# Attention, experts and a gated layer on one core: first pair's swapped keys, the experts' table and sixteen transposes moved or added

## The chip, the cores and the metric

The kernel runs on one core of a Trainium2 chip. The metric is the device time of one execution in microseconds; the profile is that of one execution of the same program. TensorE is called PE, its weight loads PEld, VectorE DVE, ScalarE ACT, GpSimd POOL and SyncE SP; "SPq" is the queue from which SP starts DMAs.

## The reference

Three stages follow each other: attention that keeps scores near the row's maximum, a layer in which each token goes to one of eight experts, and a gated layer. Sizes: batch 4, 8 heads, 576 tokens, head dimension 64; 2304 tokens of width 512; experts 512 to 1024 to 512; gated layer 512 to 1536 to 512.

```python
scores = q @ k.T / sqrt(64)
scores = where(scores >= max(scores) - tau, scores, -1e9)
x = softmax(scores) @ v                       # (2304, 512) after the heads are joined
logits = x @ w_gate
e = argmax(logits); g = softmax(logits)[e]
y = g * (relu(x @ w1[e]) @ w2[e])
out = ((y @ w_a) * (y @ w_b)) @ w_out
```

Every product is done in fp32r in two halves: a value is split into a high part (a cast to fp32r) and a low part (the value minus the high part), and three of the four partial products are summed.

## The kernel before, in words

**Attention** (class `Attention`) goes over 16 pairs of heads, i = 0 to 15: heads p and p + 4 of batch b lie in the two halves of the 128 partitions. For each pair q and k come as raw tiles of 9 blocks of 64 columns (`load`; the first pair in `__init__`, lines 296 to 298): eight blocks of the first 512 tokens and a tail with the last 64 tokens of both heads. `split_units` casts them to a high part (lines 417 to 421) and subtracts a low part (line 428). `qk_units` transposes the result on PE (lines 460, 484, 485), and ACT or DVE copies the banks into the tiles `qT` and `kT` (lines 472 to 478, 490 to 496). `kT` is kept twice, the second copy with the high and the low half of the partitions exchanged; `swap` (line 466) makes it with a DMA from the first copy. A pair then has nine score tiles, g = 9i to 9i + 8 (`s_units`): product on PE (line 677), row maximum on DVE (690), a threshold per two tiles (694), exponential on ACT (698), mask and row sum on DVE (710). `pv_units` transposes the masked weights (785), splits them (735 to 750), multiplies by v (861) and brings the heads back into rows (887).

**The gate.** After each batch `gate` computes logits, the expert of each token, its rank among the tokens of that expert (a product with a triangle matrix, lines 1002 to 1006, unit `tr`), its row in the scratch `xs` (unit `slot`, lines 1020 to 1027) and the new row counts (unit `base`, line 1037), scales the rows (`xg`) and scatters them with indirect DMAs on POOL's queue (unit `sc`, line 44). Before that, 32 zero fills (`z`, line 398) clear the rows of `xs` that may stay empty.

**The lead expert.** After three batches `lead_select` (from line 505) picks the fullest expert. Its first 256 rows are computed inside attention's last pair and behind it (`lead_units`, units `l_*`: weights, first products at line 601, second products at line 625), which gives PE work while the last gate runs.

**The order** of all of this is written out by hand: the string `ORDER` (lines 68 to 231) names every unit, and `emit` issues them in that order, so that each engine and each DMA queue gets its instructions as the string has them.

**The experts** (class `Experts`). `order` (lines 1299 to 1331) takes the counts, sorts the experts by size and builds the table `ti` with each place's expert, first output column, count and first row in `xs`; `chunk_count` computes from it how many extra chunks there are. SP, ACT and DVE read the table's values into registers (line 1605). With them SP loads an expert's rows (lines 1510 and 1512) and weights (line 1440); PE transposes the rows (line 1530), ACT and DVE split rows and weights (1532, 1533, 1446, 1447), and PE does the first (1555) and second (1576) products, eight steps an expert. 

**The gated layer** (`gated`) goes over 7 groups of one or two blocks of 128 of its 1536 columns, and in each over 5 chunks of 512 tokens (the last has 256). `front` does both products of a chunk (line 1743) and multiplies them (line 1752), and splits the result (1754, 1756); `back` multiplies by `w_out` (line 1769), one tile of 128 tokens after the other, and adds to `acc` (line 1774). In the last group each finished tile is scattered to the output (line 1776, by the helper at line 44). `back` of a chunk is issued after `front` of the next.

Of the kernel before, what the change touches and what calls it, by code (L numbers as in the profile page):

```python
# [22 lines left out]
E = 8  # L23
# [45 lines left out]
qh:0 qH:0 kh:0 kl:0 qk:0:k2 qk:0:k0 kH:0 qe:0:k2 kL:0 ql:0 qL:0 c:z qk:0:t qe:0:k0 qe:0:kt qk:0:q0 qk:0:q1 c:t qe:0:q1  # L69
qe:0:q0 qe:0:sk0 qe:0:t qe:0:sk2 s:0 qh:1 c:r ql:1 kh:1 kl:1 z:10 z:17 vh:0 vl:0 lv:1 vh:1 vl:1 c:w s:1 qk:1:t qe:1:t  # L70
qk:1:k0 qk:1:k2 m:0 e:0 m:1 e:1 th:1 p:0 s:2 p:1 s:3 m:2 m:3 qe:1:kt qe:1:k2 qe:1:k0 J:0:2 qk:1:q0 qk:1:q1 th:3 e:2
p:2 e:3 p:3 s:4 m:4 s:5 m:5 qe:1:q0 qe:1:q1 e:4 lk:2 lv:2 qe:1:sk0 pj:0 qh:2 ql:2 kh:2 kl:2 e:5 J:0:1 J:0:0 A0:0:2
A0:0:0 J:0:3 A0:0:1 Je:0 Jl:0 th:5 p:4 A0:0:3 A0e:0 s:6 p:5 s:7 m:6 m:7 e:6 th:7 p:6 A1:0:2 A1:0:0 qk:2:t A1:0:1 C:0:0
A1:0:3 s:8 e:7 z:27 qe:1:sk2 lk:3 z:12 z:28 qe:2:t A1e:0 qe:2:kt Ce:0 p:7 s:9 m:8 Cl:0 e:8 m:9 th:9 qk:2:k0 qe:2:k0
e:9 A0l:0 A1l:0 vh:2 vl:2 A3:0:3 A3:0:1 qk:2:k2 H:0:0 A3:0:0 A3:0:2 v00:0:0 H:0:1 H:0:2 A3e:0 qe:2:k2 p:8 p:9 s:10
H:0:3 s:11 m:10 m:11 B2:0:3 A2:0:3 A2:0:0 A2:0:1 A2:0:2 B2:0:2 B2:0:0 B2:0:1 He:0 Hl:0 th:11 e:10 A2e:0 A2l:0 p:10
B0:0:0 B0:0:1 B0:0:3 v00:0:1 B0:0:2 B2e:0 e:11 A3l:0 kh:3 kl:3 z:0 k:0:0 k:0:1 qk:2:q0 qk:2:q1 s:12 B0e:0 qe:2:q0
qe:2:q1 p:11 s:13 B1:0:1 B3:0:3 B3:0:0 B1:0:3 v00:0:2 rinv:0 m:12 m:13 e:12 th:13 p:12 B1:0:0 v00:0:3 J:1:0 B3:0:2
B1:0:2 v00:0:4 J:1:2 B3:0:1 J:1:3 J:1:1 e:13 v00o:0 B1e:0 p:13 s:14 v01:0:0 B2l:0 B0l:0 qh:3 pj:9 ql:3 Je:1 B3e:0
B3l:0 J2:0 B1l:0 s:15 C:1:0 v01:0:1 v01:0:2 v01:0:3 A0:1:2 v01:0:4 A0:1:0 A1:1:3 A1:1:2 A0:1:3 A0:1:1 Ce:1 m:14 m:15  # L80
Cl:1 e:14 v01o:0 e:15 x0:0 th:15 p:14 A1:1:1 s:16 A1:1:0 p:15 s:17 x0s:0 m:16 m:17 th:17 A2:1:3 A2:1:2 A2:1:1 A2:1:0
z:11 qe:2:sk2 qe:2:sk0 z:7 lk:4 z:25 lv:3 z:18 z:6 z:16 A0e:1 Jl:1 A1e:1 A0l:1 A2e:1 A2l:1 e:16 qk:3:t v10:0:0 qe:3:kt
qe:3:t v10:0:1 v10:0:2 v10:0:3 v10:0:4 qk:3:k2 qk:3:q0 qk:3:k0 e:17 p:16 p:17 rinv:1 qe:3:q0 qe:3:k0 qe:3:k2 v10o:0
# [1775 lines left out]
```

## Time and profile before

| | |
|---|---|
| median of 3 runs (lowest, highest) | 1043.4 us (1043.09, 1043.55) |
| the profiled execution's own time, its span | 1042.98 us, 1041.3 us |
| PE busy, of the span | 1003.0 us, 96% |
| DVE, ACT, POOL busy | 713.3 us (68%), 541.7 us (52%), 562.6 us (54%) |
| attention with its gates, by the timeline | from 0 to about 350 us |
| experts | to about 590 us |
| gated layer | to 1032 us, then scatters and the program's end |

The span runs from the first to the last instruction of the profile. Busy shares are averages over stages with different limits: in attention DVE, ACT and PE are all near full, in the experts and the gated layer PE alone. A row of the timeline gives the start and the duration of an instruction or of a run of like instructions, its engine and line, what it writes and reads, how many there were, and in brackets how long the engine had been idle and what ended that. Matmuls overlap in the pipeline, so that a run of eight takes less than eight times the duration of one.

### The profile page before, as it was taken

The numbers are of one execution on the slowest core, as the hardware profiler recorded it, in microseconds if no ns is written. First come the engines' busy times: TensorE is split into PE (matmuls) and PEld (weight loads), VectorE is DVE, ScalarE is ACT, GpSimd is POOL, SyncE is SP. The second block draws the span as 40 slices with busy tenths as digits, with TensorE's granted clock in tenths as the row PEclk, the third lists the DMA queues.
The fourth block names the chain that finished last, engine by engine and source line by source line (L and its number), as shares of the span: only waits on it lengthen the run. The fifth ranks groups of instructions, "written<-read, shape, count | busy, mean of one in ns | idle before, by whom it ended". The sixth has DMA issues, their size and how long they took to land.

```text
span 1041.3 us, 18663 instructions
## 1 busy us (share of the span) xinstructions
PE 1003.0 (96%) x6392; PEld 910.2 (87%) x6392; DVE 713.3 (68%) x1454; ACT 541.7 (52%) x1118; POOL 562.6 (54%) x522
## 2 busy tenths in 40 slices
PE   5899999999999899999999999999999999999996
PEld 4799999999999889999999988888888888888885
DVE  6999999999997545555599488843953945834222
ACT  4999999999996354455565344321322312321110
POOL 4888898998987521111234267633633734623334
PEclk9999999999999989999999999999999999999999
DMA  6778645445344486556666123510210310300012
GB/s 164 216 208 226 183 122 133 110 130 132 104 119 148 163 261 210 168 172 180 191 197 210 34 81 74 68 41 1 63 59 1 81 41 21 82 1 1 31 51 101
DMA packets 111777, 119.20 MB, mean 114 GB/s; under 512 B 20064, under 2 KB 82528, under 8 KB 111680
## 3 DMA queue, kind: packets, MB, share of 16 engines
q1 hardware_dynamic: 107248, 106.93, 37.0%
q0 software_dynamic: 3840, 10.50, 2.7%
q8 instruction: 51, 0.84, 0.3%
q10 hardware_dynamic: 592, 0.56, 0.2%
q14 instruction: 46, 0.38, 0.1%
HBM read 77.57 MB, written 20.98 MB: 95 GB/s over the span
## 4 chain that ended last, share of the span: by engine, by line
PE 52%; issue 5%; POOL 3%; DVE 3%; ACT 1%; POOLq 0%; DVEq 0%; ACTq 0%
PE pg L1743 22%; PE po L1769 10%; PE py_i L1576 9%; PE ph_i L1555 9%; POOL out L44 1%; PE px_i L1530 1%; POOL w L1478 1%; POOL t L1477 1%; DVE acc L1774 1%; DVE a L1469 1%; DVE w L1447 1%; POOL g L1756 0%; DVE t L1473 0%; DVE u L1470 0%; ACT w L1476 0%
## 5 line engine op out<-in xcount | busy, mean ns | idle before, releaser
L1743 PE MATMUL pg<-y,w 128*128 128x512 f32 (+1 forms) x1440 | 301.9, 368 | 0.0
L1743 PEld LDWEIGHTS pg<-y,w 128*128 128x128 f32 x1440 | 251.6, 189 | 45.3
L1756 POOL TENSOR_TENSOR g<-gg,g 128x512 fp32r<-128x512 f32 (+1 forms) x58 | 76.2, 1314 | 151.0 <-ACT g L1754 150.9
L1769 PE MATMUL po<-w,g 128*128 128x512 f32 x648 | 153.3, 390 | 0.6 <-DVE acc L1774 0.6
L1769 PEld LDWEIGHTS po<-w,g 128*128 128x128 f32 x648 | 120.9, 188 | 26.2 <-issue 0.8
L1447 POOL TENSOR_TENSOR w<-raw,w 128x512 fp32r<-128x512 f32 x33 | 45.3, 1373 | 160.5 <-ACT w L1446 154.3
L750 POOL TENSOR_TENSOR pt<-st,pt 128x512 fp32r<-128x512 f32 x93 | 119.8, 1295 | 10.1 <-ACT pt L740 7.2
L1754 ACT CAST g<-gg 128x512 fp32r<-128x512 f32 (+1 forms) x60 | 34.7, 578 | 170.1 <-PE po L1769 97.3
L1555 PE MATMUL ph_i<-xt_i,w 128*128 128x256 f32 (+4 forms) x768 | 118.9, 302 | 4.3 <-DVE w L1447 2.4
L1752 DVE TENSOR_TENSOR gg<-ga,pg 128x512 f32<-128x512 f32 (+1 forms) x60 | 37.7, 629 | 122.0 <-PE pg L1743 122.0
L1576 PE MATMUL py_i<-h_i,w 128*128 128x256 f32 (+4 forms) x768 | 114.0, 297 | 0.3 <-PEq L1670 0.3
L1555 PEld LDWEIGHTS ph_i<-xt_i,w 128*128 128x128 f32 x768 | 106.9, 192 | 6.0 <-DVE w L1447 3.1
L1576 PEld LDWEIGHTS py_i<-h_i,w 128*128 128x128 f32 x768 | 106.5, 192 | 0.7 <-ACT w L1446 0.6
L861 PE MATMUL pv<-pt,sv 128*128 128x288 f32 x512 | 103.3, 317 | 0.2 <-ACT o L866 0.2
L1774 DVE TENSOR_TENSOR acc<-acc,po 128x512 f32<-128x512 f32 x108 | 72.7, 683 | 34.6 <-PE po L1769 34.6
L785 PE MATMUL tp<-idf,P 128*128 128x128 f32 x504 | 89.9, 274 | 2.2 <-DVE P L710 1.3
L1477 POOL TENSOR_TENSOR t<-t,w 128x512 f32<-128x512 f32 x36 | 53.2, 1478 | 64.0 <-ACT w L1476 47.7
L1446 ACT CAST w<-raw 128x512 fp32r<-128x512 f32 x128 | 75.7, 618 | 15.0 <-PE py_i L1576 5.9
L1447 DVE TENSOR_TENSOR w<-raw,w 128x512 fp32r<-128x512 f32 x95 | 68.3, 730 | 11.0 <-ACT w L1446 9.0
L861 PEld LDWEIGHTS pv<-pt,sv 128*128 128x128 f32 x512 | 75.0, 190 | 0.8 <-ACT o L866 0.6
L1560 DVE SCALAR_TENSOR_TENSOR h_i<-ph_i,h_i 128x256 fp32r<-128x256 f32 (+4 forms) x64 | 28.8, 451 | 62.5 <-ACT h_i L1559 62.5
L1559 ACT ACTIVATE h_i<-ph_i 128x256 fp32r<-128x256 f32 (+4 forms) x64 | 26.1, 407 | 83.5 <-PE ph_i L1555 62.7
(249 smaller groups left out, 1920.0 us busy)
## 6 DMA issues: line engine op xcount, KB each, us to landing
raw<-in_moe_w SPq DMA_DIRECT2D x128, 256.0 KB
xs<-zero SPq DMA_DIRECT2D x32, 320.0 KB
tk<-half SPq DMA_DIRECT2D x64, 144.0 KB
raw<-in_moe_w_a SPq DMA_DIRECT2D x12, 512.0 KB
raw<-in_moe_w_b SPq DMA_DIRECT2D x12, 512.0 KB
raw<-in_moe_w_out SPq DMA_DIRECT2D x12, 512.0 KB
kT<-kT SPq DMA_DIRECT2D x32, 160.0 KB
kT<-kT SPq DMA_DIRECT2D x30, 144.0 KB
```

The source lines that it names most:

```text
L750: nc.gpsimd.tensor_sub(lo, st, fr(hi))
L785: nc.tensor.transpose(st["ps"][:, 128 * j:128 * j + 128], parts(j), idf)
L861: nc.tensor.matmul(R["v", n][:, 0:HALF], lhs, z, start=(c == 0 and r == 0), stop=(c == 4))
L1446: nc.scalar.copy(hi_t, raw)
L1447: engine.tensor_sub(lo_t, raw, fr(hi_t))
L1477: g.tensor_sub(t, t, fr(hi))
L1555: nc.tensor.matmul(ps[:, 0:n], w[a][:, k, :], xt[b][k][:, 0:n], start=(s_ == 0), stop=(s_ == len(steps) - 1))
L1576: nc.tensor.matmul(st["y"][d][:, 0:n], w[a][:, 0, d * P:d * P + P], h[b][:, 0:n], start=(f == 0 and d % each == 0 and (a, b) == (0, 0)), s ...
L1743: mm = nc.tensor.matmul(ps[:, 0:n], w[g][j][m][a][:, k, :], self.y[b][:, k, c0:c0 + n], start=(s_ == 0), stop=(s_ == len(steps) - 1))
L1756: last = low.tensor_sub(gl[:, 0:n], gt[:, 0:n], fr(gh)[:, 0:n])
L1769: nc.tensor.matmul(ps, res[j][a][:, t * P:t * P + P], w[g][j][2][b][:, 0, :], start=(s_ == 0), stop=(s_ == len(steps) - 1))
L1774: nc.vector.tensor_tensor(acc[:, tt, :], acc[:, tt, :], ps, op=ALU.add)
```

## The change

It has six parts.

1. **Ahead of all**, sixteen transposes of the identity on PE into a bank that nothing reads.
2. **The start.** The exchanged copy of the first pair's keys is no longer made by a DMA. ACT casts the raw keys a second time beside the first pair of halves (POOL for the tail), so that a tile holds high, low, high; transposing blocks two and three of it gives the exchanged copy, which ACT and DVE copy into `kT`. The tails of q and k come as four loads, q's from ACT's queue, and POOL splits them. The zeros move from DVE to POOL, `tau` from ACT's queue to SP's, and the constants (units `c:r`, `c:m`) go ahead of the first casts on DVE.
3. **The table** of `order` moves into the last gate: counts in `base`, ranking in `places`, the table in `table`, most of it on a PSUM bank; what does not depend on the last batch is done in `lead_select`. `base` no longer waits for `slot`.
4. **The end.** In the last chunk the second block's split result has buffers of its own, and the last tile is done in two halves of 256 columns.
5. **`ORDER`** is written anew from end to end, with eight more units.
6. The planner's list of dependencies in `run` follows.

```diff
 ORDER = """
-qh:0 qH:0 kh:0 kl:0 qk:0:k2 qk:0:k0 kH:0 qe:0:k2 kL:0 ql:0 qL:0 c:z qk:0:t qe:0:k0 qe:0:kt qk:0:q0 qk:0:q1 c:t qe:0:q1
-qe:0:q0 qe:0:sk0 qe:0:t qe:0:sk2 s:0 qh:1 c:r ql:1 kh:1 kl:1 z:10 z:17 vh:0 vl:0 lv:1 vh:1 vl:1 c:w s:1 qk:1:t qe:1:t
+c:r c:m kh:0 qh:0 k3:0 kl:0 kH:0 qH:0 kL:0 qL:0 K3:0 qk:0:t qk:0:k0 qe:0:ks qe:0:k0 qk:0:k2 c:z qk:0:sk0 qk:0:sk2 ql:0
+c:t qe:0:k2 qk:0:q0 qk:0:q1 qe:0:sk2 qe:0:q1 qe:0:t qe:0:sk0 qe:0:kt lk:2 kh:1 kl:1 vh:0 vl:0 qh:1 ql:1 qe:0:q0 s:0
...
+Hl:3 v11o:2 A2e:3 B0:3:0 B0e:3 z:21 lk:6 z:5 z:8 lv:5 A1l:3 kh:6 kl:6 B0l:3 pj:36 k:3:0 z:31 z:25 z:12 qe:5:sk2
...
+g:gate:15 l_ap:2 l_ah:2 l_ad:2 l_b:1 tr:gate:15 l_hint slot:gate:15 base:gate:15 l_wh:4:1 l_wd:4:1 l_wl:5:0 l_wh:5:0
+xg0:gate:15 l_wd:5:0 l_wl:5:1 l_wh:5:1 l_wd:5:1 xg3:gate:15 l_ap:3 l_ah:3 l_ad:3 places:gate:15 l_b:2 xg1:gate:15
+xg2:gate:15 l_ap:4 l_ah:4 xh:gate:15 table:gate:15 l_ad:4 l_b:3 l_ap:5 sc0:gate:15 sc1:gate:15 sc2:gate:15 sc3:gate:15
...
         for n in "kq":
-            nc.sync.dma_start(self.state[0]["raw_" + n][:, 8, :], two[n][:, 512:576].rearrange("a s d -> a s d"))
+            for a in range(2):
+                (nc.sync if n == "k" else nc.scalar).dma_start(self.state[0]["raw_" + n][64 * a:64 * a + 64, 8, :], two[n][a, 512:576])
...
+        idle = self.psV.tile([P, 512], F32, tag="V", name="idle")
+        for _ in range(16):
+            nc.tensor.transpose(idle[:, 0:P], consts["idf"], consts["idf"])
...
         def zeros():
             for z in self.qj:
-                nc.vector.memset(fr(z), 0.0)
-            nc.vector.memset(self.z, 0.0)
+                nc.gpsimd.memset(fr(z), 0.0)
+            nc.gpsimd.memset(self.z, 0.0)
...
+        def again(z):
+            def run():
+                o, x = s["sk"][:, z, 2, :], s["raw_k"][:, z]
+                if z == tail:
+                    nc.gpsimd.tensor_scalar(o, x, 1.0, 1.0, op0=ALU.mult, op1=ALU.mult)
+                else:
+                    nc.scalar.copy(o, x)
+            return run
...
+        def again(n):
+            def front():
+                if "S" not in ps:
+                    ps["S"] = self.psS.tile([P, 2, 512], F32R, tag="S", name="again")
+                for j in range(4):
+                    nc.tensor.transpose(ps["S"][:, n, P * j:P * j + P], kb(4 * n + j, 1), idr)
+
+            def back():
+                (nc.vector.tensor_copy if n else nc.scalar.copy)(tile("kT")[:, 1, 640 * n:640 * n + 512], flat(ps["S"])[:, n])
+            return front, back
...
+            if last:
+                counts[:] = cnt, key, G2 = bank(112, E), bank(120, E), bank(128, E * E)
+                v.tensor_tensor(cnt, pre[:, 5], r["rest"], op=ALU.add)
...
+        def places():
+            cnt, key, G2, rk, M, st = *counts, bank(104, E), bank(192, E * E), bank(48, E)
+            row, col = lambda z: z.unsqueeze(1).to_broadcast([P, E, E]), lambda z: z.unsqueeze(2).to_broadcast([P, E, E])
+            v.tensor_reduce(rk, grid(G2), axis=AX.X, op=ALU.add)
+            v.tensor_tensor(grid(G2), grid(G2), row(r["src"][:, 2, :]), op=ALU.mult)
+            v.tensor_tensor(grid(M), row(rk), col(r["io"]), op=ALU.is_equal)
+            v.tensor_reduce(st, grid(G2), axis=AX.X, op=ALU.add)
+            v.tensor_scalar(r["src"][:, 1, :], st, r["kept"], None, op0=ALU.add)
+
+        def table():
+            big = bank(256, 4 * E * E).rearrange("p (z a b) -> p z a b", z=4, a=E)
+            shape = [P, 4, E, E]
+            v.tensor_tensor(big, grid(bank(192, E * E)).unsqueeze(1).to_broadcast(shape), r["src"].unsqueeze(2).to_broadcast(shape), op=ALU.mult)
+            with nc.allow_low_precision(reason="one whole number and zeros"):
+                v.tensor_reduce(r["ti"], big, axis=AX.X, op=ALU.add)
+            v.tensor_reduce(r["T"], big, axis=AX.X, op=ALU.add)
+            v.tensor_copy(r["st"], bank(48, E))
+            self.psT.done(G["pr"])
...
+                    need.update(base=["tr"], places=["base"], table=["places", "slot"])
...
-    def order(self):
...
+                    end = (g, c0) == (ng - 1, chunks[-1][0])
+                    if end and j:
+                        gh, gl = [self.cv.tile([P, 512], F32R, tag=z, name=f"g_{z}") for z in ("mag", "t")]
...
+                    wide = DM // 2 if (g, tt) == (ng - 1, ntile - 1) else DM
+                    for z in range(0, DM, wide):
+                        z = slice(z, z + wide)
+                        for s_, (j, a, b) in enumerate(steps):
+                            nc.tensor.matmul(ps[:, z], res[j][a][:, t * P:t * P + P], w[g][j][2][b][:, 0, z],
+                                             start=(s_ == 0), stop=(s_ == len(steps) - 1))
...
-    ex.order()
```

In the string, `qk:0:sk0` and `qk:0:sk2` are the transposes of the exchanged keys, `qe:0:sk0`, `qe:0:sk2` and `qe:0:ks` their copies (before, `qe:0:sk0` and `qe:0:sk2` were the DMAs), `k3:0` and `K3:0` the second casts, `z` a zero fill, `k:3:0` a DMA that stacks halves of pair 3, `l_ap` and `l_b` the lead expert's first and second products, `l_wl`, `l_wh` and `l_wd` the load, cast and subtraction of its weights. Around the score tiles 39 and 40 the new string has the fills 21, 5, 8, 31, 25, 12, 26, 24, 20, 14 and 17 on SP's queue, in between the loads of pairs 5 and 6, the swaps of pair 5 and the two stacked tiles of pair 3; the old one had four fills there (19, 21, 14, 30).

## Rows read from the trace of the kernel before

**Rows 1.** Stretches: busy us and instructions of each engine, PEclk, DMA share, GB/s
```profile
0.00:26.03 26.03, 13.21 (x71) 11.72 (x71) 18.03 (x57) 10.88 (x22) 12.04 (x31) 1.00 0.62 164
78.09:104.10 26.01, 26.01 (x215) 25.46 (x214) 24.79 (x59) 24.80 (x51) 22.29 (x23) 1.00 0.80 226
338.39:364.40 26.01, 21.52 (x173) 20.87 (x173) 14.80 (x46) 8.02 (x17) 15.46 (x16) 0.94 0.49 163
364.42:390.50 26.08, 24.02 (x134) 22.75 (x132) 12.42 (x26) 13.63 (x28) 6.48 (x5) 0.86 0.81 261
```

**Rows 2.** Waits of SP's queue, 340 to 380 us: total us, times, longest
```profile
SPq L1605 <- DVE o_ti L1331: 7.2, 1, 7.2
```

**Rows 3.** Timeline of the start, 0 to 23 us
```profile
1.70 0.40 DVE L1803 CAST idr<-idf 128x128 fp32r<-128x128 f32 x1 [0.76 <-POOL idf masks.py:199]
...
4.06 0.69 DVE L428 TENSOR_TENSOR sk<-raw_k,sk 128x512 fp32r<-128x512 f32 x1
...
5.78 0.20 DVE L417 CAST sk<-raw_k 128x64 fp32r<-128x64 f32 x1 [1.03 <-DMA raw_k<-in_k]
...
6.86 0.24 ACT L419 CAST sq<-raw_q 128x64 fp32r<-128x64 f32 x1 [1.90 <-DMA raw_q<-in_q]
...
7.79 1.22 PE L460 MATMUL tq<-idr,sq 128*128 128x128 f32 x8
...
9.62 1.41 POOL L428 TENSOR_TENSOR sk<-raw,sk 128x576 fp32r<-128x576 f32 x1
...
9.71 1.35 DVE L1280 CAST io<-io_int 128x8 f32<-128x8 int32 x1
...
12.68 0.16 DVE L359 TENSOR_SCALAR base<-io 128x8 f32<-128x8 f32 x1
...
14.48 1.81 PE L677 MATMUL S_J<-kT,qj 128*128 128x288 f32 x6 [3.99 <-DMA kT<-kT]
...
16.33 0.76 DVE L690 TENSOR_REDUCE mt<-S_J 128x1 f32<-128x576 f32 x1 [0.35 <-PE S_J L677]
...
22.00 0.25 POOL L717 TENSOR_SCALAR J<-J 128x64 f32<-128x64 f32 x1
```

**Rows 4.** Timeline of PE, 31 to 40 us
```profile
31.70 1.33 PE L677 MATMUL S_J<-kT,qj 128*128 128x288 f32 x8
...
39.01 0.87 PE L460 MATMUL tq<-idr,sq 128*128 128x128 f32 x8
```

**Rows 5.** Timeline of the hand-over, 342 to 373 us
```profile
342.64 0.24 PE L1006 MATMUL tr<-oh,ones 128*128 128x40 bf16 x4
...
351.82 0.99 POOL L44 DMA_INDIRECT xs<-xg,si  x1 [0.30 <-issue]
...
356.69 0.70 DVE L1331 CAST o_ti<-o_T 128x32 int32<-128x32 f32 x1
...
358.53 0.37 SPq L1510 DMA_DIRECT2D xr_i<-xs  x1
...
362.49 2.58 PE L1530 MATMUL px_i<-idf,xr_i 128*128 128x128 f32 x12 [2.56 <-DMA xr_i<-xs]
...
366.83 6.23 PE L1555 MATMUL ph_i<-xt_i,w 128*128 128x352 f32 x24 [1.76 <-ACT w L1446]
```

**Rows 6.** Timeline of the end, 1028 to 1036 us
```profile
1028.31 0.69 DVE L1774 TENSOR_TENSOR acc<-acc,po 128x512 f32<-128x512 f32 x1 [0.67 <-PE po L1769]
...
1029.67 0.69 DVE L1774 TENSOR_TENSOR acc<-acc,po 128x512 f32<-128x512 f32 x1
...
1032.16 1.28 DVE L1774 TENSOR_TENSOR acc<-acc,po 128x512 f32<-128x512 f32 x2 [1.80 <-PE po L1769]
...
1034.41 0.98 POOL L44 DMA_INDIRECT out<-acc,i_idc  x1 [0.30 <-issue]
```

**Rows 7.** The tile of the results, 1027 to 1042 us: its transfers
```profile
DMA to landing us min/median/max: 2.7/2.7/3.0
```

**Rows 8.** The page's DMA issues: the zero fills
```profile
xs<-zero SPq DMA_DIRECT2D x32, 320.0 KB
```

More of the change, by code (lines that the diff above doesn't have):

```diff
@@ L74 @@
[L74 to L83, printed above, removed]
@@ L342, in rest, with more @@
                 )
+        def more():
+            i2, ji = tiles["i2"], tiles["ji"]
+            routing.update(routing.pop("late")())
             nc.vector.tensor_copy(self.II, i2.unsqueeze(1).to_broadcast([P, 2, D]))
@@ L365, in wide @@
             nc.vector.tensor_copy(self.WT[:, :, W:WT], self.W2[:, 4:8, D:W])
-        self.setup = {"t": scales, "z": zeros, "r": rest, "w": wide}
+        self.setup = {"t": scales, "z": zeros, "r": rest, "w": wide, "m": more}
     def load(self, i, names):
@@ L426, in run @@
                 t = s["s" + n][:, z]
-                g = nc.vector if n != "v" and (i, n) in self.FIRST else nc.gpsimd
+                g = nc.vector if n != "v" and (i, n) in self.FIRST and not (i == 0 and z == tail) else nc.gpsimd
                 g.tensor_sub(t[:, :, 1, :], s["raw_" + n][:, z], fr(t)[:, :, 0, :])
@@ L482, in tails, with again_tail @@
         def tails():
-            t = ps["t"] = self.psT.take(F32R, f"tt{i}", 2)
+            t = ps["t"] = self.psT.take(F32R, f"tt{i}", 2 + (i == 0))
             nc.tensor.transpose(t[:, 0:P], qb(8), idr)
             nc.tensor.transpose(t[:, P:2 * P], kb(8), idr)
+            if i == 0:
+                nc.tensor.transpose(t[:, 2 * P:3 * P], kb(8, 1), idr)
+        def again(n):
[7 more added lines that the diff above has]
+            return front, back
+        def again_tail():
+            t = fr(ps["t"])
+            nc.scalar.copy(tile("kT")[:, 1, 512:640], t[:, 2 * P:3 * P])
+            nc.scalar.copy(tile("kT")[:, 1, 1152:1216], t[:, 2 * P + 64:3 * P])
+            self.psT.done(ps["t"])
         def tails_evac():
@@ L520, in lead_select @@
         v.tensor_scalar(r["kept"], top[:, 0:1], float(LEAD), float(LEAD), op0=ALU.is_ge, op1=ALU.mult)
+        v.tensor_scalar(cnt, r["sel"], r["kept"], None, op0=ALU.mult)
+        v.tensor_tensor(r["src"][:, 3, :], cnt, r["eb"], op=ALU.add)
+        v.tensor_tensor(r["rest"], ps[:, 112:112 + E], r["src"][:, 3, :], op=ALU.subtract)
         self.psT.done(ps)
@@ L1038, in bases @@
                 self.psT.done(G["pr"])
+        grid = lambda z: z.rearrange("p (a b) -> p a b", a=E)
+        if last:
+            bank = lambda lo, m: G["pr"][:, lo:lo + m]
+            counts = [None] * 3
+        def places():
[15 more added lines that the diff above has]
+            self.psT.done(G["pr"])
         def scaled(t):
@@ L1065, in gate @@
         return [("lt", tail), ("tl", sum_tail), ("L", logits), ("top", top), ("shift", shifted), ("ex", exps),
-                ("tr", ranks), ("g", weight), ("slot", slots), ("base", bases), *[(f"xg{t}", scaled(t)) for t in range(4)], ("xh", scaled_tail),
+                ("tr", ranks), ("g", weight), ("slot", slots), ("base", bases), *((("places", places), ("table", table)) if last else ()), *[(f"xg{t}", scaled(t)) for t in range(4)], ("xh", scaled_tail),
                 *[(f"sc{t}", rows(t)) for t in range(5)]]
@@ L1173, in run @@
                     at((k, "gate", i), T("gate"), f, *prev)
-                at(("gate", i), T("gate"), lambda: None, ("base", "gate", i))
+                at(("gate", i), T("gate"), lambda: None, ("table" if i == n - 1 else "base", "gate", i))
         end = 9 * n
@@ L1813, in attention_experts_gated @@
         sel=c.tile([P, E], F32, name="sel"),
+        rest=c.tile([P, E], F32, name="rest"),
+        st=c.tile([P, E], F32, name="st"),
+        T=c.tile([P, 4, E], F32, name="T"),
+        ti=c.tile([P, 4, E], I32, name="ti"),
         kept=c.tile([P, 1], F32, name="kept"),
```

404 lines of the change are left out of this document (196 added, 208 removed).

## The prediction

> **What bounds the kernel now.** I read four views. The stretches come first [rows 1]: in the middle of attention TensorE (PE) is busy 26.01 of 26.01 us, beside DVE with 24.79 and ACT with 24.80, so there all three work at the same pace and little can be won; PE idles at the start (13.21 busy of 26.03) and where attention hands over to the experts (21.52 of 26.01, then 24.02 of 26.08). In the two stretches of the hand-over the granted clock is 0.94 and 0.86. The waits of SP's queue name what the hand-over hangs on [rows 2]: 7.2 us for `o_ti`, the table of the experts' rows. The timeline of the start, of the hand-over and of the end gives the terms [rows 3 to 6]. The rest (the experts, the gated part) is PE after PE and is not touched.
>
> The sum stands against the profiled execution: span 1041.3, its own time 1042.98, 0.4 below the median of 1043.4. I take the gain off the median. A measurement here can tell about 0.2% (2.1 us) from no change.
>
> **The start.** Before, the last tails of k and q reach their casts at 5.78 and 6.86, PE transposes until 9.0 (7.79 + 1.22), the first product can only begin, waits 3.99 for the swap, goes on at 14.48, and DVE's first maximum stands at 16.33 [rows 3]. After it there is no such DMA: nine more transposes of k with its halves exchanged, copied out by ACT and DVE. Step by step:
> - The tails go out as four loads, q's two on ACT's queue behind two loads instead of fourth on SP's. I take 6.3 for the later one, between 5.78 and 6.86.
> - Five small POOL instructions cast and subtract them. The nearest row is 0.25 us for 128x64 [rows 3]; four follow the later tail, with subtractions somewhat longer: 1.1, so PE can begin at 7.4 (6.8 to 8.2).
> - PE then does 27 transposes in a row. Eight took 1.22 us at the start and 0.87 at 39 us [rows 3, 4]: 4.1 or 2.9 us, so to 11.5 or 10.3. Evacuations run along; that of the last swapped bank ends with the last transpose.
> - The first product has eight matmuls: 6 took 1.81 at 14.48 (8 would take 2.3), 8 took 1.33 at 31.70. The first maximum comes at 13.8 or 11.7, against 16.33: a gain of 2.5 or 4.6.
>
> Here is the choice. [...] Before, PE idled most of the first 14 us; after, sixteen transposes run from the identity on (its copy is cast at 1.70) and 27 from 7.4. I take the clock as up part of the way: 3.5. The rounds of products and masks up to 22 us then run faster too: of the 13.21 us that PE is busy in the first stretch I put 6 between the first maximum and 22 us; at 1.6 times the later duration 2.3 of them go, and I count half, since only the products lie in the loop of product, maximum and mask: 1.0 (0 to 2.4). **The start gives 4.5** (2.5 to 7.0), and PE, full from 40 us on, carries it.
>
> Costed at nothing: the sixteen transposes themselves (1.7 us by the rate at 39 us, 2.4 by that of the start, more if a transpose of f32 takes longer) end before 6, while PE waits for the tails until 7.4; their bank is next written by the first weighted sum. ACT's second cast of k, no longer than the 0.69 of the subtraction beside it, fits before PE asks. The constants that DVE now does ahead of its first casts took 9.71 to 12.84, 3.1 us [rows 3]; from 2.10, where the identity's copy ends, they put the first casts' start at 5.2 and their end, two of at most 0.7, at 6.6, still under the cover of the tails (7.4). Without that cover they'd cost 6.6 less the 4.75 at which that subtraction ended before, 1.9. The zeros move from DVE to POOL, behind the tails, where POOL's next work, pair 1's subtraction, began only at 9.62. SP loses the two swaps and gets one small load and tau; its next loads move by under 1 us.
>
> [...] A DVE cast of 128x8 at 9.71 took 1.35 us, just as long as POOL's subtraction at 9.62 still ran; the last of that run took 0.16 [rows 3]. [...]
>
> **The middle.** The written order is new from end to end but keeps the same operations and prefetch distances. 0, with 3 either way (1% of 300 us), as nothing in the trace shows which order is better.
>
> **The hand-over.** Before, the last ranks are at 342.64, the table's last cast ends at 357.39, SP sends the first expert's rows at 358.53, they are on PE at 362.49 after 2.56 idle, and the first product follows at 366.83 [rows 5]. After, counts, places and table stand in the last gate on PSUM tiles, ahead of the lead expert's last casts. It is fourteen small DVE instructions; at half of the 0.70 of the table's cast each, an estimate, they end 5 us behind the ranks instead of 14.8, and at the full 0.70 still 10 behind. That takes `o_ti` off the path: SP's 7.2 us go [rows 2]. What is late next is the last scatter: it was issued at 351.82, and a scatter lands 2.7 behind its start [rows 7]; with the register loads done meanwhile, the rows could go at 354.5 to 355.5, 3.0 to 4.0 earlier. The ranks also stand one lead product earlier in the order (1.6), and weights and scatters follow them: up to 1.5 more. PE's lead work, which ended at 359.93 (362.49 less 2.56), is then last: behind the ranks it grows by that product and loses the stalls that the late table made among the lead's casts. So the wait of 2.56 goes, and about 2 of stalls: **4.5**. [...]
>
> **The end.** The adds of the last tiles came 1.36 apart until 1029.67; then two came together at 1032.16, and the last scatter began at 1034.41 [rows 6]. In the last chunk three buffers serve four results, so that one waits until the previous chunk is read. With a buffer of its own, tile 16 can be added and scattered 1.1 earlier, and the last tile's second half needs an add of half the columns, about 0.4 in place of 0.64 (two took 1.28). Its scatter then begins at 1033.3, 0.3 behind the one before: **1.1** (0 to 1.3). The matmuls' columns are the same.
>
> **The sum:** 4.5 + 0 + 4.5 + 1.1 = 10.1; 1043.4 - 10.1 = 1033.3.
>
> **The rivals.**
> - *The clock does not follow.* The early transposes don't raise it and it falls at the hand-over as before. For: the fall there and the slow start. Start 2.5, hand-over 3.0, end 1.1: 1036.8.
> - *Weights bound the hand-over.* Six loads of 256 KB go out behind the rows, and the first product waited for a cast of one of them; against: they move up with the rows. Hand-over 1.5: 1036.3.
> - *It does not do what it says.* The middle loses what the ends win, since PE, DVE and ACT are all near full there and the order is new: 3% of 300 us is 9: about 1043.
> - *Slower: the zero fills.* Behind product 39 the new order puts eleven fills of 320 KB, nine of them ahead of pair 3's last stacked tile and six ahead of pair 5's swaps; the old one had four there. At 226 GB/s [rows 1, 8] one takes 1.45, nine take 13.0. If nothing covers them, PE waits 13.0: 1046.3. It decides from 10.1 us uncovered on. Against: pair 5's first product, 45, is six tiles of work later, and PE was busy without a gap from 78 to 104 us, where transfers ran at that rate.
>
> **How the numbers follow.** Forecast 0.60, clock 0.18, weights 0.10, nothing won 0.06, slower 0.06. The forecast's own bounds reach from 1027.6 (7.0 + 7.5 + 1.3) to 1039.4 (2.5 + 1.5 + 0); both middle rivals lie inside, so the range is 1027.5 to 1040.0. Faster by over 0.2%: 0.60, 0.18 and 0.10 less 0.01 for their tails: 0.87; slower: 0.06 and a hundredth of the order's spread: 0.07; same: 0.06.
>
> **What would show it.** The first maximum at 12 to 14 us and no PE wait on kT; products of 128x288 at their later pace before 15 us; SP without a wait on the table, PE idle under 1 us ahead of the first expert's rows and a clock of 1.00 there; last adds 1.36 apart. Wrong it is if the middle between the first maximum and the last ranks is longer by over 3 us, or if the first expert's product still starts over 24 us behind the ranks.

## The result and the profile after

The changed kernel takes 1030.38 us as the median of 4 runs (1028.2 to 1031.99) against 1043.47 of the kernel before (4 runs, 1043.09 to 1044.2): ratio 0.9872, 95% interval 0.985 to 0.9895, 13.1 us faster. Predicted were 1033.3 in 1027.5 to 1040.0. The profiled execution after took 1031.99, with a span of 1030.3: the longest of its four, and 10.99 below the 1042.98 of the profiled execution before. Measured twice more, the same kernel took 1029.78 (0.9869, 0.985 to 0.9888) and 1029.65 (0.9872, 0.9852 to 0.9893).

The stretches of the profile after, columns as in [rows 1]:

```profile
0.00:26.00 26.00, 18.22 (x112) 15.99 (x112) 20.20 (x59) 16.26 (x35) 18.48 (x42) 1.00 0.62 168
78.00:104.00 26.00, 25.98 (x213) 25.24 (x212) 24.61 (x59) 24.61 (x51) 21.70 (x23) 1.00 0.73 205
338.00:364.00 26.00, 25.59 (x189) 24.50 (x188) 13.10 (x34) 11.38 (x24) 14.82 (x15) 1.00 0.72 235
364.00:390.00 26.00, 24.24 (x138) 22.37 (x137) 12.65 (x27) 11.87 (x24) 3.91 (x3) 0.93 0.73 226
```

PE is busier at the start and in the first stretch of the hand-over (25.59 us at a clock of 1.00, where [rows 1] has 21.52 at 0.94). The next stretch still loses: 24.24 busy and a clock of 0.93. Full attention is as full as it was.

**The start**, the timeline that answers to [rows 3]:

```profile
1.72 3.68 PE L306 MATMUL idle<-idf 128*128 128x128 f32 x16 [1.72 <-POOL idf masks.py:199]
...
3.94 0.41 DVE L438 CAST sk<-raw_k 128x512 fp32r<-128x512 f32 x1
...
6.29 0.31 POOL L449 TENSOR_TENSOR sq<-raw_q,sq 128x64 fp32r<-128x64 f32 x1
...
6.66 0.37 PE L506 MATMUL tt<-idr,sq 128*128 128x128 f32 x1 [1.26 <-POOL sq L449]
6.69 1.11 DVE L332 COPY mt<-tau_abs 128x12 f32<-128x12 f32 x1
6.75 0.55 POOL L336 MEMSET qj<- 128x256 f32 x2
...
7.08 1.22 PE L482 MATMUL tq<-idr,sk 128*128 128x128 f32 x8
...
8.09 1.22 PE L516 MATMUL again<-idr,sk 128*128 128x128 f32 x8
...
10.88 2.05 PE L723 MATMUL S_J<-kT,qj 128*128 128x288 f32 x7 [0.19 <-ACT kT L536]
...
12.72 0.82 PE L723 MATMUL S_A<-kT,qT 128*128 128x288 f32 x4
12.96 0.76 DVE L736 TENSOR_REDUCE mt<-S_J 128x1 f32<-128x576 f32 x1 [0.61 <-PE S_J L723]
...
43.68 0.45 DVE L941 TENSOR_TENSOR x<-tx,rinv 128x288 f32<-128x288 f32 x1
```

The last row's counterpart in the profile before:

```profile
47.89 0.45 DVE L895 TENSOR_TENSOR x<-tx,rinv 128x288 f32<-128x288 f32 x1
```

The first maximum stands at 12.96 instead of 16.33, 3.4 earlier. The swap's 3.99 are gone; PE waits 0.19 for a copy instead. In this execution all 27 transposes run at the pace of 1.22 for eight and seven products take 2.05; from 12.72 on four products take 0.82. So here the faster pace (0.82 for four) comes only as the first maximum does, and the rounds behind it gain from it: the first masked exponential stands at 18.26 instead of 22.86 (4.6), the first pair's x, the weighted sum of its values, at 43.68 instead of 47.89 (4.2).

**The hand-over**, the waits of SP's queue from 340 to 380 us, where [rows 2] had 7.2 for `o_ti`:

```profile
SPq L1718 <- SPq L1718: 3.8, 1, 3.8
...
SPq L1558 <- DMA xs<-xg,si: 2.5, 1, 2.5
```

and the timeline that answers to [rows 5]:

```profile
336.22 0.24 PE L1052 MATMUL tr<-oh,ones 128*128 128x40 bf16 x4
...
340.91 0.42 DVE L1113 TENSOR_REDUCE ti<-tr 128x32 int32<-128x256 f32 x1
...
344.42 0.98 POOL L44 DMA_INDIRECT xs<-xh,si  x1 [0.30 <-issue]
...
347.49 0.37 SPq L1558 DMA_DIRECT2D xr_i<-xs  x1
...
351.45 1.67 PE L1578 MATMUL px_i<-idf,xr_i 128*128 128x128 f32 x12
...
354.45 4.38 PE L1603 MATMUL ph_i<-xt_i,w 128*128 128x352 f32 x24
...
360.06 10.23 SPq L1488 DMA_DIRECT2D raw<-in_moe_w  x10
...
365.61 1.34 ACT L1494 CAST w<-raw 128x512 fp32r<-128x512 f32 x2 [5.25 <-DMA raw<-in_moe_w]
...
366.28 3.22 PE L1603 MATMUL ph_i<-xt_i,w 128*128 128x352 f32 x12 [1.62 <-ACT w L1494]
```

The ranks are 6.4 earlier, the table ends 5.1 behind them, the rows go out 11.0 earlier, and PE comes to them without a wait. The first expert's product starts at 354.45 instead of 366.83, 12.4 earlier, and its 24 matmuls take 4.38 instead of 6.23. Then PE waits 1.62 for the fourth pair of weights, whose loads SP sent at 360.06, and the clock falls behind that (stretches of 2 us):

```profile
368.00:370.00 2.00, 2.00 (x9) 2.00 (x8) 0.78 (x3) 0.99 (x3) 1.31 (x1) 0.50 1.00 310
370.00:372.00 2.00, 2.00 (x10) 1.48 (x9) 1.97 (x5) 1.45 (x3) 0.00 (x0) 0.65 0.91 258
```

The second expert's first `h_i`, after and before:

```profile
390.56 0.44 ACT L1607 ACTIVATE h_i<-ph_i 128x320 fp32r<-128x320 f32 x1 [2.20 <-PE ph_i L1603]
```
```profile
400.97 0.44 ACT L1559 ACTIVATE h_i<-ph_i 128x320 fp32r<-128x320 f32 x1 [2.20 <-PE ph_i L1555]
```

There the lead is 10.4, and it is 10.5 at the first add of the gated layer (632.03 instead of 642.54). In between each of the two executions has one fall of the clock to 0.50 (from 569.5 before, from 559.1 after), so that the lead stays as it is.

**The end**, the timeline that answers to [rows 6]:

```profile
1015.12 0.69 DVE L1829 TENSOR_TENSOR acc<-acc,po 128x512 f32<-128x512 f32 x1
...
1020.57 1.13 DVE L1829 TENSOR_TENSOR acc<-acc,po 128x512 f32<-128x512 f32 x2 [0.67 <-PE po L1824]
...
1021.75 0.62 PE L1824 MATMUL po<-w,g 128*128 128x256 f32 x3 [0.51 <-DVE acc L1829]
...
1022.77 0.42 DVE L1829 TENSOR_TENSOR acc<-acc,po 128x256 f32<-128x256 f32 x1 [1.07 <-PE po L1824]
...
1023.47 0.98 POOL L44 DMA_INDIRECT out<-acc,i_idc  x1 [0.96 <-DVE acc L1829]
```

Five adds are 1.36 apart now, but the last tile's second half waits 0.51 for the add of its first half. The last scatter stands at 1023.47 instead of 1034.41, 10.9 earlier, where the first of these adds is 10.5 earlier (1015.12 for 1025.59): the end adds 0.5.

### The profile page after: what moved, and what is told of

Its sections match the earlier page's. It is cut to its first block, busy times and chain, and to the rows that moved or that the text cites. A ratio compares the mean times of both kernels' runs of the same rounds, so it can differ in the third digit from the quotient of the medians.

```text
span 1030.3 us, 18735 instructions
## 1 busy us (share of the span) xinstructions
PE 1004.6 (98%) x6423; PEld 911.4 (88%) x6423; DVE 711.7 (69%) x1453; ACT 541.2 (53%) x1121; POOL 564.3 (55%) x530
## 4 chain that ended last, share of the span: by engine, by line
PE 52%; issue 5%; POOL 3%; DVE 3%; ACT 1%; DMA 1%; POOLq 0%; SPq 0%; DVEq 0%; ACTq 0%
PE pg L1791 22%; PE po L1824 11%; PE py_i L1624 9%; PE ph_i L1603 9%; POOL out L44 1%; PE px_i L1578 1%; POOL w L1526 1%; POOL t L1525 1%; DVE w L1495 1%; DMA raw<-in_moe_w 1%; DVE acc L1829 1%; DVE a L1517 1%; POOL g L1808 0%; DVE t L1521 0%; DVE u L1518 0%
## 5 line engine op out<-in xcount | busy, mean ns | idle before, releaser
L1829 DVE TENSOR_TENSOR acc<-acc,po 128x512 f32<-128x512 f32 (+1 forms) x109 | 73.0, 679 | 34.4 <-PE po L1824 34.3
```

The source lines that it names most:

```text
L1829: nc.vector.tensor_tensor(acc[:, tt, z], acc[:, tt, z], ps[:, z], op=ALU.add)
```

## The experiments

All are the changed kernel with the edit named, unless it says otherwise. "Ranks" is the group of rank matmuls, as in [rows 5]. Times are medians of 4 to 6 runs, or one run where no interval stands; the last three columns are read from one profile of each.

| kernel | us | ratio, interval | first maximum | ranks | first add, gated |
|---|---|---|---|---|---|
| before | 1043.47 | | 16.33 | 342.64 | 642.54 |
| after | 1030.38 | 0.9872, 0.985 to 0.9895 | 12.96 | 336.22 | 632.03 |
| after_again | 1029.78 | 0.9869, 0.985 to 0.9888 | 11.47 | 337.09 | 629.66 |
| after_third | 1029.65 | 0.9872, 0.9852 to 0.9893 | 13.02 | 336.26 | 628.40 |
| no_sixteen | 1031.05 | 0.989, 0.9865 to 0.9915 | 12.83 | 336.72 | 631.00 |
| no_sixteen_again | 1033.44 | 0.9904, 0.9885 to 0.9922 | 12.91 | 338.35 | 633.39 |
| swap_by_dma | 1035.23 | 0.9926, 0.9909 to 0.9944 | 15.89 | 341.16 | 633.61 |
| late_table | 1038.80 | 0.9954, 0.9937 to 0.997 | 13.18 | 337.66 | 639.52 |
| fourth_ahead | 1028.77 | 0.9868, 0.9831 to 0.9905 | 11.35 | 334.90 | 625.91 |
| whole_last | 1030.73 | | 12.28 | 336.38 | 631.27 |
| two_banks | 1030.68 | | 12.16 | 338.38 | 631.34 |
| before_sixteen | 1042.46 | | 16.34 | 341.64 | 641.85 |
| both | 1027.18 | 0.9846, 0.9828 to 0.9864 | 12.28 | 337.60 | 630.74 |
| both_24 | 1027.74 | 0.9862, 0.9839 to 0.9885 | 11.47 | 336.49 | 627.75 |

Four groups were measured side by side, each on one chip: after_again, no_sixteen, swap_by_dma and late_table; fourth_ahead, whole_last, two_banks and before_sixteen; after_third, no_sixteen_again and both; both_24 by itself.

**The changed kernel again.** No edit.

> The changed kernel as it is, once more, because its four times lay 3.8 us apart (1028.2 to 1032.0) and the profiled one was among the longest. [...] Rival: the spread comes from attention; then the last ranks are at another time than 336.2, by 2 us or more, and the hand-over takes as long as before. Time 1028 to 1032.5, ratio 0.9850 to 0.9895.

The profiled execution took 1029.62, 2.37 less than the first. Its first maximum is 1.5 earlier, but the clock stands at 0.50 from 23.2 to 30.0 us, where the first profile has no fall, and its ranks are 0.9 later. Yet the second expert's first `h_i` is 0.9 earlier: PE's wait for the fourth weights is 0.44 instead of 1.62 and no clock falls there. The other 1.5 come near 560 us, where both idle 1.9 us for a cast of weights but only the first one's clock falls behind it (0.93 against 1.00 in the stretch from 546 to 572). The third profile, of a time near the other end (1028.34), makes the cleaner pair: its ranks are at the same place (336.26 against 336.22), and of its 3.65 us 2.2 lie in the hand-over and 1.5 behind 560. So the spread is in part at the hand-over, with the wait for the fourth weights and the fall behind it, and in part in a second place, behind 560; and behind the start too the clock falls in one of the three profiles and not in the others.

> The changed kernel as it is, beside the next two on one chip, so that their differences of 1 to 3 us are taken against it and not against other calls. 1029 to 1031 as the middle; single times from 1027 to 1032, as the eight so far.

Its stretches from 364 and from 546 us, with no wait for the fourth weights and no fall in either place:

```profile
364.00:390.00 26.00, 26.00 (x160) 24.76 (x160) 14.24 (x30) 13.25 (x27) 4.03 (x4) 1.00 0.83 259
546.00:572.00 26.00, 24.07 (x199) 23.73 (x198) 20.64 (x38) 12.64 (x28) 8.10 (x5) 1.00 0.46 143
```

**Without the sixteen transposes.**

```diff
-        idle = self.psV.tile([P, 512], F32, tag="V", name="idle")
-        for _ in range(16):
-            nc.tensor.transpose(idle[:, 0:P], consts["idf"], consts["idf"])
```

> The changed kernel without the sixteen transposes of the identity. In its profile PE's first product runs at the slow pace until the first maximum at 12.96, and only behind it at the later pace, where the kernel before kept the slow one until about 22. Theory: the 27 transposes of k and q from 6.66 on are work enough by themselves; the first maximum stays at 13.0 and the first masked exponential at 18.3, both within 0.3, and the time is within 1 us of the changed kernel's 1030.4. Rival: the sixteen are what brings the later pace on so early; then the products stay slow up to some 9 us behind the first transpose, as in the kernel before (14.48 to about 23), that is to 15.5 or 16; the first maximum is still at 13.0, the first masked exponential comes 0.5 to 1.2 later, and the time is 0.5 to 1.5 longer.

> The changed kernel without the sixteen transposes, with more rounds. In the profiles with them the first maximum came between 11.35 and 13.18 and x of the first pair between 42.1 and 44.4; in the one without, at 12.83 and 43.8. [...]

The start's timeline without them:

```profile
10.74 2.05 PE L720 MATMUL S_J<-kT,qj 128*128 128x288 f32 x7 [0.19 <-ACT kT L533]
...
12.83 0.76 DVE L733 TENSOR_REDUCE mt<-S_J 128x1 f32<-128x576 f32 x1 [0.61 <-PE S_J L720]
```

The same pace and the same wait as with them, and the first maximum 0.13 earlier than in the first profile; the first masked exponential is at 18.4 against 18.26. So the 3.4 us of the start in the first profile owe nothing to the sixteen. The time is longer all the same, by 1.3 against after_again and by 3.8 against after_third; over all runs, thirteen with them have a mean of 1029.8 and ten without 1032.6. The rival of the first run puts such a loss into the start, and there these two profiles do not show it: the second one without them loses its 2.1 by the ranks (x of the first pair at 43.62, as with them) and has a fall of the clock in the hand-over. What the sixteen do shows in other profiles: in four of the nine of the changed kernel and its variants that have sixteen, the eight transposes of k take 0.84 instead of 1.22, in the two without never. But the early pace does not always last: in whole_last and two_banks the clock falls at 8.55 and in after_again at 23.2, and of the four only fourth_ahead keeps it (x at 42.12). Over the eight with the early swap x comes at 42.1 to 44.4, without the sixteen at 43.6 and 43.8. Why the runs without them are longer by more than that stays open.

**The swap by DMA again.**

```diff
-c:r c:m kh:0 qh:0 k3:0 kl:0 kH:0 qH:0 kL:0 qL:0 K3:0 qk:0:t qk:0:k0 qe:0:ks qe:0:k0 qk:0:k2 c:z qk:0:sk0 qk:0:sk2 ql:0
-c:t qe:0:k2 qk:0:q0 qk:0:q1 qe:0:sk2 qe:0:q1 qe:0:t qe:0:sk0 qe:0:kt lk:2 ...
+c:r c:m kh:0 qh:0 kl:0 kH:0 qH:0 kL:0 qL:0 qk:0:t qk:0:k0 qe:0:kt qe:0:k0 qe:0:sk0 qk:0:k2 c:z ql:0
+c:t qe:0:k2 qe:0:sk2 qk:0:q0 qk:0:q1 qe:0:q1 qe:0:t lk:2 ...
...
```

> The changed kernel with the first pair's swapped k made by two DMAs from the transposed k, as in the kernel before, and without the third copy of k, its two casts and its nine transposes; the sixteen transposes, the split tail loads, the order of the setup and all else stay. Theory: the first product waits for the swap again, the first maximum comes at 15.5 to 16.5 instead of 12.96, the clock stays at the lower level to 20 us or later, and the 3.5 to 4.5 us last to the end: the time is 3 to 5 us longer. Rival: attention behind the start is bound by DVE and ACT as much as by PE and takes the delay up; then the last ranks are within 1 us of 336.2 and the time is within 1.5 us.

```profile
14.08 1.78 PE L718 MATMUL S_J<-kT,qj 128*128 128x288 f32 x6 [2.43 <-DMA kT<-kT]
...
15.89 0.76 DVE L731 TENSOR_REDUCE mt<-S_J 128x1 f32<-128x576 f32 x1 [3.55 <-PE S_J L718]
```

The wait for the swap is back. Against after_again the maximum is 4.4 later, x 3.6 (46.93), the ranks 4.1, the profiled execution 4.0 and the median 5.4: the theory, the median a little above its 3 to 5. Attention takes none of it up.

**The table late.**

```diff
-... l_ap:3 l_ah:3 l_ad:3 places:gate:15 l_b:2 ... xh:gate:15 table:gate:15 l_ad:4 ...
+... l_ap:7 l_ah:7 l_ad:7 places:gate:15 table:gate:15 gate:15 l_b:6 l_b:7 l_y ...
```

> The changed kernel with the experts' places and table moved in the written order behind the lead expert's last cast of h, about where the kernel before had them; same instructions, same PSUM tiles. Theory: the table is then the last thing that SP waits for again. DVE's last cast of h began at 350.41, so the table is ready at 353 and the first expert's rows go out at about 353.5 instead of 347.5; PE stands idle for 2 to 3 us ahead of the rows, the first expert's product starts 5 to 6 us later than 354.45, the time is 3 to 6 us longer. Rival: weights, scatters and the branch of the chunk loop bound the hand-over anyway, and the early table buys little; then the product at 366 still starts within 1 us of where it was and the time is within 1.5 us.

The hand-over's timeline and one stretch of it:

```profile
353.91 0.42 DVE L1113 TENSOR_REDUCE ti<-tr 128x32 int32<-128x256 f32 x1
...
355.31 0.37 SPq L1558 DMA_DIRECT2D xr_i<-xs  x1
...
359.64 2.58 PE L1578 MATMUL px_i<-idf,xr_i 128*128 128x128 f32 x12 [5.44 <-DMA xr_i<-xs]
```
```profile
358.00:362.00 4.00, 2.36 (x12) 2.31 (x12) 0.00 (x0) 0.10 (x1) 0.00 (x0) 0.50 0.98 347
```

9.0 us longer than after_again, twice what the forecast gave for the hand-over. The table bounds it again, as the theory says, but the theory's price was short: PE is idle for 5.44 ahead of the rows and for 1.8 more ahead of the first product, for a cast of weights, and the clock stands at 0.50 from 358 to 370, where the twelve transposes of the rows take 2.58 instead of 1.67. This is not the kernel before in every respect: there PE's lead work ended later, and the idle time was 2.56.

**The fourth weights ahead of the branch.**

```diff
+            for m in range(2):
+                w0[3].load(m)
             self.chunks()
```

> The changed kernel with the two loads of the first expert's fourth pair of weights issued ahead of the branch of the chunk loop instead of behind it; the six raw buffers stay, so SP waits for the first casts before it reaches the branch. Theory: the 2 us that the hand-over gives back (12.4 us earlier at the first expert's first product, 10.4 from its sixth h on) come from those loads, which stand behind SP's 3.8 us at the branch and the next expert's rows: they land at 365.6, PE waits 1.62 for their cast and can fall to the lower clock behind it. With them ahead, PE idles under 0.5 us between 362 and 368, the gain at the later h stays at 11.5 to 12.4 in the profile's terms, and the time is 1 to 3 us shorter: 1027.5 to 1029. Rival: the fifth pair, whose loads go no earlier, is late in its place, or SP is held up by the wait ahead of the branch; then PE waits as long one product later and the time is within 1 us of 1030.2.

```profile
348.89 6.63 SPq L1488 DMA_DIRECT2D raw<-in_moe_w  x8
...
353.69 4.34 PE L1603 MATMUL ph_i<-xt_i,w 128*128 128x352 f32 x24
...
362.09 3.68 PE L1603 MATMUL ph_i<-xt_i,w 128*128 128x352 f32 x22
```

The third and fourth pairs' 22 matmuls now follow each other without a wait, and PE is busy 26.00 of 26.00 us from 364 to 390 at a clock of 1.00. The fifth pair is not late. One profile without the wait does not show by itself that the edit took it away, since after_third has none either: of the eight profiles with the early table and these loads behind the branch, five have the wait (0.44 to 1.85) and three have none. Of the three with the loads ahead (this one, `both` and `both_24`) none has it, and their hand-over, from the ranks to the second expert's first `h_i`, is 6.7 to 7.3 shorter than the kernel before's, that of the eight 3.3 to 7.4. As to time, the profiled execution has the earliest marks of all (1025.86); the other three (1028.27 to 1030.48) are no better than the changed kernel's, and the interval is too wide for more.

**The last tile in one piece, or in two banks.**

```diff
-                    wide = DM // 2 if (g, tt) == (ng - 1, ntile - 1) else DM
+                    wide = DM
```

> The changed kernel with the last tile of the output in one piece of 512 columns again; the sixth pair of buffers for its low parts stays. Theory: the second half's matmuls waited 0.51 for the add of the first half, which stands behind the add of the tile before on DVE and frees the bank that both halves share; in one piece the six matmuls follow at 1.36, the last add begins 1.25 behind the one before it and takes 0.69, and the last scatter begins about 1.25 to 1.36 behind the one before it instead of 1.94: 0.6 to 0.7 us shorter from the first add of the last five to the last scatter (7.65 instead of 8.35). Rival: the halves save their part of the add as they are and the wait costs nothing net; then this stretch is 0.2 to 0.4 longer.

```profile
1021.15 0.69 DVE L1829 TENSOR_TENSOR acc<-acc,po 128x512 f32<-128x512 f32 x1 [0.67 <-PE po L1824]
...
1022.12 0.98 POOL L44 DMA_INDIRECT out<-acc,i_idc  x1 [0.38 <-DVE acc L1829]
```

From the first of the last adds (1014.35) to the last scatter it is 7.77, against 8.35 with the halves and 8.82 before (1025.59 to 1034.41): the second block's own buffers win 1.05, and the halves lose 0.58 of it again.

```diff
                     for z in range(0, DM, wide):
+                        if z:
+                            ps = self.psy.tile([P, 512], F32, tag=f"y{(tt + 1) % 4}", name=f"pz_{g}_{tt}")
                         z = slice(z, z + wide)
```

> The changed kernel with the second half of the last tile in a PSUM bank of its own (that of the tile three before it, which is read by then). Theory, as for the piece in one: the halves wait for each other only because they share a bank; with two banks PE goes on without the 0.51, the second half's add of 0.42 ends about 1.3 behind the add before the first half's, and the last scatter follows the one before it without a gap: the stretch from the first add of the last five to the last scatter is 7.3 to 7.5 instead of 8.35. Rival: the second half still waits for the first half's add (the accumulator's row, or DVE's queue), and it is 8.2 or more.

```profile
1020.38 0.52 PE L1826 MATMUL pz<-w,g 128*128 128x256 f32 x3
...
1021.30 0.42 DVE L1831 TENSOR_TENSOR acc<-acc,pz 128x256 f32<-128x256 f32 x1 [0.29 <-PE pz L1826]
1022.12 0.99 POOL L44 DMA_INDIRECT out<-acc,i_idc  x1 [0.30 <-issue]
```

With banks of their own the halves no longer wait, and the add is done at 1021.72; but the scatter queue needs 0.98 and 0.30 of issue for each tile, and the stretch is 7.69 (1014.43 to 1022.12). The expectation of 7.3 to 7.5 left the 0.30 out. Halves are worth 0.08 at best.

**The sixteen in the kernel before.** The loop that no_sixteen takes out, added there.

> The kernel before with the sixteen transposes of the identity ahead of all and nothing else of the change. Theory: they run while PE waits for the first tails, PE then stands idle for 4 us ahead of the swap as before, and what the sixteen may have brought on is lost there: first maximum at 16.3 within 0.3, the later pace from about 23 us on, time within 1.5 us of 1043.5. Rival: the sixteen keep the pace up through the wait; then products are at the later pace before 18 us, the first masked exponential comes 1 us or more before 22.9, and the time is 1 to 2.5 us shorter.

First maximum 16.34, first masked exponential 22.87, time 1042.46 in its one run: nothing in the start, where PE idles for the swap behind them. Its clock stands at 0.65 in the stretch from 8 to 12 us and at 0.50 from 12 to 20.

**The two edits together**, fourth_ahead and whole_last.

> The changed kernel with the fourth pair's loads ahead of the branch and the last tile in one piece, the two edits that took a wait away. Theory: the two add up: 2 us at the hand-over, up to 1.7 more where the changed kernel's clock falls behind that wait, and 0.6 at the end: 2.5 to 4 us shorter than the changed kernel beside it, 1026 to 1028. Rival: what the early loads won in the one profile (1025.86) was that execution's clock, as its other three times of 1028.3 to 1030.5 would have it; then the two kernels differ by 0.5 to 1.2, the end's part.

1027.18 against the changed kernel's 1029.65 on the same chip: 2.5 shorter by the medians, at the theory's lower end, with four of five runs between 1026.91 and 1027.26. The two intervals overlap, so this pair alone does not settle it. Together with the next kernel, which has the same two edits, nine runs have a mean of 1027.9, against 1029.8 for the thirteen of the changed kernel: it is faster, by about 2. Of the two parts the end's is shown (7.76 from the first of the last adds to the last scatter, as in whole_last); what the loads give is not separated from the spread.

**Twenty-four instead of sixteen**, on top of that.

> The kernel with the two edits, and twenty-four transposes of the identity instead of sixteen, so that PE is busy until about the time at which k's and q's tails come (6.5 to 6.9) instead of standing idle for 1.1 to 1.5 us ahead of them. At 0.22 each they end at 7.1, at 0.11 from 5.2 on at 6.3. Theory: the level that the sixteen bring on at 5.1 to 6.1 in some executions is lost again in that idle time, and with it the 1.5 us between a first maximum at 11.4 and one at 12.2 to 13.2; here the maximum comes at 11.2 to 11.6 in the profile and the times lie 0.5 to 1.5 below those of the kernel with sixteen (1027.18 as the middle): 1025.5 to 1026.7. Rival: the level is not to be had that early in every execution, and where it is not the eight more transposes hold the tails up by 0.4; the maximum is at 12.3 to 13.5 and the time is the same within 0.5 or longer.

```profile
1.72 4.41 PE L306 MATMUL idle<-idf 128*128 128x128 f32 x24 [1.72 <-POOL idf masks.py:199]
...
6.99 0.84 PE L482 MATMUL tq<-idr,sk 128*128 128x128 f32 x8
...
10.07 1.20 PE L723 MATMUL S_J<-kT,qj 128*128 128x288 f32 x7 [0.69 <-ACT kT L536]
...
11.47 0.75 DVE L736 TENSOR_REDUCE mt<-S_J 128x1 f32<-128x576 f32 x1
```

The maximum is at 11.47, as the theory has it, and x at 42.23, 2.0 earlier than in `both`; the time, on another chip, is not shorter: 1027.74 against 1027.18. The earlier start is not to be found in it.

## Why the prediction was right, and where not

The range held, and the likeliest case was the right one. That the removed swap, the early table and the end's own buffers are the causes is shown by swap_by_dma, late_table and whole_last. By its steps, in the profiled execution (4.2 + 2.2 + 4.1 + 0.5 = 11.0, of 10.99):

- *The start, 3.5 at the first maximum and 1.0 behind it.* Measured 3.4 and 1.2, of which 4.2 reach x. The size was right and the mixture wrong. That the clock would be up "part of the way" was the author's estimate, and no run shows it for the transposes of k: here they all ran at 1.22 for eight, in after_again at 0.84, where the maximum came 4.9 earlier than before, in after_third as here. By execution it was the one pace or the other, and 3.5 met the one that was profiled. The 1.0 behind the maximum took the products at 1.6 times their later duration, an estimate too; in this execution four products took 0.82 from 12.72 on, in the kernel before 1.16 at 16.09. PE began at 6.66 and not at 7.4, because the later tail was there before 5.29, where its cast began, and not at 6.3; that made up for it. swap_by_dma shows the removed swap as the cause (3.6 us at x), and no_sixteen that the transposes ahead have no part in the 3.4.
- *Costed at nothing.* The sixteen end at 5.39, under the wait for the tails, and the first cast of k, put at 5.2 behind the constants, was on DVE at 3.94. Nothing of that was late. But "nothing" was not the price of taking the sixteen away: the runs without are 1.3 and 3.8 longer, in a way that no profile here places.
- *POOL and DVE.* A copy of 128x12 took 1.11 at 6.69 and ended at 7.80, with POOL's fills of `qj` and `zero` (6.75 to 7.77); in the kernel before, with POOL idle, the same copy took 0.17. So it lasted as long as the fills beside it, as the cast at 9.71 lasted as long as POOL's subtraction [rows 3]; what makes it last is not shown. Nobody waited for that copy, and the sum lost nothing by it.
- *The middle, 0 with 3 either way.* The profiled execution has 2.2, which looks like a gain of the new order. It is within the spread: from the first x to the ranks the twelve profiles of the changed kernel and its variants take 292.2 to 294.7 (mean 293.5), the two of the kernel before 294.7 and 294.1. No run has the old order with the rest of the change.
- *The hand-over, 4.5.* Measured 4.1, from 6.4 at the ranks to 10.5 at the gated layer. That it came so near is luck: up to the second expert's first `h_i` this profile has 4.0, after_again 5.8 and after_third 6.2. On the way it was 12.4 at the first expert's product. The table ended 5.1 behind the ranks (5 was said), the last scatter was next (rows 3.07 behind its start, 2.7 was said), the wait of 2.56 went. The step that failed is what comes after: the clock was to stay at 1.00 or the weights to bind from the first product on. Neither: the first three pairs were in time, the fourth was not, since its loads stand behind SP's 3.8 us at the branch. PE's wait of 1.62 there and the fall of the clock gave 2.0 back. With the loads ahead the wait is in none of three profiles. So a part of the rival "weights bound the hand-over" was true, three products later than it said. The 1.5 and 7.5 that the range takes as the bounds of the hand-over were the author's estimates, and no run shows them; from the ranks to the second expert's first `h_i` the profiles with the early table gained 3.3 to 7.4.
- *The end, 1.1.* Measured 0.5. The step "the last tile's second half needs an add of half the columns" forgot that both halves lie in one PSUM bank: the second half's matmuls wait for the first half's add (0.51), and in two_banks they do not. whole_last measures the term without it, 1.05.
- *The rivals.* "The clock does not follow" was right for the first 12 us of this execution and wrong for the sum, and the zero fills cost nothing: PE is busy 25.98 of 26.00 us from 78 to 104.
- *From 1033.3 to 1030.4.* 1032.4 is what the prediction's base less 10.99 gives. The rest is that the profiled execution was the longest of four: two falls of the clock, at 368 and at 560, are in it and not in others, 3.65 us in the pair of profiles with equal ranks. By the same steps after_again gives 4.6 + 1.0 + 5.8 + 0.5 and after_third 3.9 + 2.5 + 6.2 + 0.5, and each 1.6 more behind 560, where the kernel before has the fall in both of its profiles: 13.4 and 14.6 in all. The prediction had put nothing on that stretch.

## What to carry to other kernels

In late_table a wait of 5.44, and the weights' 1.8 behind it, made 9.0, with the granted clock at 0.50 from 358 to 370: taking off the path what an idle engine waited for was worth more than the wait. After such a step look for the next load in the same queue, here the fourth pair of weights behind a branch, and move that too. And splitting the last tile did not help here: with the halves in one bank it cost 0.58, and in two, where the scatter queue was already full, it gave 0.08.

## What was not expected of the hardware

- One kernel, one input, and the clock takes different ways: the seven products of the first row take 2.05 in one profile of the changed kernel and 1.19 in the next, and the same 1.9 us of idle time near 557 us is followed by a fall of the granted clock (to 0.50 from 559.1 on in the first profile) in 6 of the 12 profiles of it and its variants and by none in the others. A fall was worth about 1.5 us here.
- In both_24 the pace rose with transposes alone. Nothing but transposes ran on PE before 9.0, the first six took 1.54, nine from 4.97 on took 1.16, and the eight of k took 0.84, where the first profile of the changed kernel has 1.22.
- The column of the granted clock says 1.00 from the start of every profile until the first fall is on record, also where eight transposes take 1.22. At the start the pace of equal instructions has to be read instead.
- SP's branch around the chunk loop took 3.8 us, from 353.93 to 357.74, for a loop whose body did not run. Over the fourteen profiles it took 0.5 to 3.8, and where it was short SP then waited for loads that it had sent before (1.0 and 2.4 in `both`), so that a shorter branch alone need not send the next loads earlier. The trace shows neither the cause nor why the time differs.
